# Nine half-chunk loads of a gated mix kernel, each as one transfer in place of two, under a new order of issue

## The chip, the cores and the metric

The kernel runs on one core of one Trainium2 chip. Times are device microseconds (us) of that core from start to end of an execution. Five engines work side by side, each on a list of instructions of its own that it takes strictly in order: PE (TensorE, matmuls), ACT (ScalarE), DVE (VectorE), POOL (GpSimd) and SP (SyncE, which here does nothing but issue transfers between the chip's memory and the on-chip memory of 128 partitions). Sixteen DMA engines carry out the transfers. Engines wait for each other and for transfers through semaphores. A lower time is better.

## The reference

Two branches over the same `x` (2048 rows of 640), mixed by a gate for each row:

```python
g = sigmoid((x * gate_w).sum(-1, keepdims=True))
# A: 32 heads of 20; each position attends to 8 positions back, two apart
qkv = x @ wqkv                      # 640 x 1920
a = softmax(q.k * scale over 8 positions) . v, then @ wo        # 640 x 640
# B: two dense layers with mish between them
h = x @ w1 + b1                     # 640 x 1728
b = (h * tanh(softplus(h))) @ w2    # 1728 x 640
out = g * a + (1 - g) * b
```

All of it is in float32. The hidden width of B is 1728 = 13 chunks of 128 and a last chunk of 64: that last half chunk is what the change is about.

## The kernel before, in words

**Arithmetic.** Every matmul operand is held as a pair of tiles, a high part (rounded) and a low part (what the rounding left), and every product is three matmuls: high by high, high by low, low by high (`mm3`, lines 522 to 524). The first layer of B, the projections and `wo` use a Strassen-like scheme of seven products in place of eight; the second layer (`mlp2`) does so over the halves of the hidden width and of the output: seven products `a b c e g d f`, each over seven chunks of the hidden width.

**What a load is.** A chunk (128 partitions by 256 to 512 columns, so 128 to 256 KB) is fetched by a transfer that SP issues, into a `raw`, `z` or `hb` buffer or straight into a `pair` buffer. ACT copies it to the high part (line 463). DVE or POOL subtracts to get the low part (line 466). Only then can PE read it. In the stretch of `mlp2` each step needs one chunk of weights and two of activations (`act`, `actt`, which the first layer has written to the chip's memory).

**The half chunk.** Products b, g and f end with a chunk of only FR = 64 rows. There the kernel puts the 64 rows twice into the 128 partitions and lets one matmul do the work of two: the high weights stand below the low ones, so two matmuls (lines 1401 and 1402) replace three. `load_low_w` fetches such weights (three times), `load_low_act` such activations (six times: products b, g, f by two halves P of the rows). Both fetch through `twice` (line 1199), which issues the same 64 rows as two transfers, one to partitions 0 to 63 and one to partitions 64 to 127 (line 1203). In `load_low_w`, line 1211 is ACT's high part, 1212 DVE's low part, 1214 the second copy by ACT and 1215 a clearing by POOL.

**What sets the order.** The code records 2856 tasks with their dependencies and buffers. A table written out by hand, `ISSUE`, gives for each of the five engines the order of its task numbers; a second table, `TAKEN`, gives for each ring of buffers which engine takes the next one. `Plan.run` walks the tables and emits the instructions in just that order; tasks marked for either engine run on DVE or POOL, whichever list they stand in. Nothing reorders afterwards. An engine that comes to a task whose inputs are not there waits, and all that stands behind it in its list waits too. SP's list is the order in which all transfers are issued.

**Other transfers that matter below.** `placed_unit` moves a border of the key and value tile by two transfers, one of 112 partitions and one of 15 (`kv[112:127]`), eight times for each of two widths. `make_gates` stores gates by transfers of 8 partitions, eight in all. All other transfers have 128, 64, 32 or 16 rows. In the program of before, the first dimension of a transfer is always its number of partitions or rows.

Of the kernel before, what the change touches and what calls it, by code (L numbers as in the profile page):

```python
# [22 lines left out]
FR = F - FC * 128  # L23
# [43 lines left out]
class Task:  # L67
# [8 lines left out]
    "PE": """1 96-110 115 120 125 135 130 145 140 244 240 236 232 290 263 302 294 267 298 376 377 380 381 383 385 425 426 386 429 387 430  # L76
487 432 434 488 435 491 456 436 492 494 496 468 464 497 498 460 540 548 544 536 619 620 623 624 626 628 650 629 630 651 654
655 657 659 681 660 724 661 725 728 689 729 693 685 731 733 734 767 735 759 755 763 878 921 894 922 925 1047 1046 1049 926
928 930-932 1048 1063 1089 1064 1090 1066 1092 1065 1107 1091 1108 1125 1109 1203 1204 1127 1110 1126 1207 1208 1128 1210
1212-1214 1234 1235 1338 1238 1339 1239 1241 1243-1245 1340 1289 1371 1341 1290 1372 1391 1373 1293 1294 1374 1392 1296 1298  # L80
1299 1394 1300 1459 1460 1393 1505 1463 1464 1506 1466 1468 1509 1469 1470 1510 1515 1517-1519 1542-1544 1559 1545 1560 1562
1583 1581 1561 1597 1595 1631 1582 1584 1632 1596 1633 1609 1611 1634 1598 1610 1612 1729 1658 1730 1657 1660 1880 1659 1732
1881 1731 1882-1891 1901 1902 1927 1928 1938 1939 1973-1984 2026-2037 2047 2048 2060 2061 2071 2072 2098-2109 2137-2144 2151
2152 2162 2163 2173 2174 2190-2197 2239-2246 2265 2266 2276 2277 2287 2288 2307-2314 2337-2348 2358 2359 2371 2372 2382 2383
2402-2413 2446-2457 2467 2468 2478 2479 2489 2490 2506-2517 2543-2550 2557 2558 2570-2573 2674 2574-2578 2675 2679 2579 2695
2580 2581 2680 2684 2696 2686 2700 2701 2689 2692 2705 2707 2806 2729 2710 2831 2733 2713 2807 2832 2811 2836 2828 2837 2812
2816 2841 2843 2818 2846 2821 2824 2849 2853""",
    "ACT": """7 4 10 13 19 16 31 22 25 28 47 38 41 35 44 116 126 111 62 127 121 78 74 122 59 117 118 136 112 50 72 123 128 131 119 228 124
# [12 lines left out]
1246 1237 1359 1367 1161 1388 1368 1248 1249 1257 1387 1004 1164 1375-1377 1369 1292 1291 1251 1378 1379 1007 1380 1381 1370  # L101
# [16 lines left out]
2779 2730 2734 2833 2781 2756 2785 2827 2753 2759 2789 2829 2787 2815 2840 2817 2842 2852 2854""",  # L118
    "DVE": """0 8 5 14 20 11 17 23 26 32 29 48 39 42 36 45 68-70 63 60 51 73 75 57 54 161 162 164 165 185 167 186 168 188 91 155 189 278
170 171 191 360 172-175 93 176 192 177 371 283 178 364 179 194-196 392 197 311 312 398 198 199 401 314 441 315 200 201 317  # L120
202 318 447 335 336 424 203 320 503 321-323 509 338 339 324-326 341 342 327 328 344 345 516 557 558 329 560 635 346 606 618
641 561 347 644 913 348 666 563 349 350 564 351 672 352 581 582 566 567 353 568 569 584 585 570 740 571 851 828 587 746 857
588 572-574 590 591 853 592 871 593 890 594 595 776 777 855 899 779 780 596 597 937 782 1056 575 598 943 800 1103 941 783
801 1121 954 785 786 599 787 963 803 788 804 789 790 806 791 807 792 993 793 1334 794 1027 1156 1219 1225 1157 1159 1346 809
810 1160 811 1018 1150 1354 1347 1355 1250 812 1162 1256 813 1356 1163 1348 814-816 1349 1165 817 1166 818 1167 1168 1357
1169 1170 1180 1305 1311 1181 1171 1183 1184 1172 1173 1412 1475 1481 1186 1187 1413 1174 1415 1416 1524 1529 1418 1189-1194
1419 1195-1197 1436 1640 1198 1636 1437 1421-1423 1638 1642 1637 1424-1426 1641 1639 1427 1643 1439 1440 1428 1951 1429 1430
1942 1666 1442 1842 1443 1852 1667 1669 1670 1445-1447 1931 1448-1454 1672 2004 2051 2040 1673 1690 1691 1995 1675 1998 1693
1676 1694 1677 1678 2043 1679-1681 2087 1696 1682 1683 1697 2124 2158 1750 1699 2147 2136 1700 1751 1701 1684 2155 2161 2150
1702 2294 2177 1703 1704 2207 2189 1705 2183 1753 1754 2272 2216 1706 2275 2283 1707 1756 2300 2094 2297 1708 1757 2333 2324  # L130
1774 1775 2327 1759 1760 2357 2351 1761 2598 2392 1762 2362 2330 2354 2224 2367 1763 2499 1764 2414 2561 2416 2389 2418 2381
# [198 lines left out]
def kernel(ctx: ExitStack, tc: tile.TileContext, x, wq, wo, w1, b1, w2, out):  # L330
    nc = tc.nc
# [59 lines left out]
    add = plan.add  # L391
# [808 lines left out]
    def twice(to, src, after=()):  # L1200
        def both():
            for a in (0, FR):
                nc.sync.dma_start(to.at(slice(a, a + FR)), src())
# [587 lines left out]
```

## Time and profile before

| what | value |
|---|---|
| time, median of 3 runs | 612.4 us (611.7 to 614.93) |
| time of the profiled execution | 615.71 us |
| its span, first to last instruction | 613.9 us |
| matmuls | 2645, granted clock 1.00 |
| PE busy | 605.7 us, 99% of the span |
| DVE, ACT, POOL busy | 566.4, 402.5, 396.2 us |
| bytes moved | 164.20 MB |
| transfers issued | 758 by SP, 12 by POOL |

The span is what the engines show; the 1.8 us between it and the time of that execution lie before the first and after the last instruction. The profiled execution was 3.3 us longer than the median. Rows of waits read "who waits <- whom: us in total, times, longest". Rows of a chain of waits read "start, length, what". Rows by stretch of time give, for each engine, its busy us and in brackets its number of instructions, then the granted clock, the mean busy share of the 16 DMA engines and GB/s. PE's busy time includes matmuls that are pipelined, so the count of matmuls in a stretch tells more of its pace than its busy time.

### The profile page before, as it was taken

The page shows a single profiled execution, that of the slowest core. Times are in us where ns is not written, and L with a number is a line of the kernel's source. Part 1 is how long each engine was busy: PE and PEld are TensorE (multiplying, and loading weights), DVE is VectorE, ACT ScalarE, POOL GpSimd, SP SyncE. Part 2 cuts the span into 40 slices and gives each one's busy share as a digit, 9 for nine tenths or more (in the row PEclk, how much of TensorE's full clock was granted, in tenths as well). Part 3 has the DMA queues.
Part 4 walks back from the last instruction along what each step waited for, and adds up shares of the span by engine and source line. Part 5 has one row for each costly group of instructions (what it writes and reads, how often), then busy time and mean ns, then how long its engine had stood idle before and what let it go on. Part 6 is the DMA issues. An engine that isn't in the chain of part 4 may idle for free.

```text
span 613.9 us, 9016 instructions
## 1 busy us (share of the span) xinstructions
PE 605.7 (99%) x2645; PEld 495.3 (81%) x2645; DVE 566.4 (92%) x513; ACT 402.5 (66%) x902; POOL 396.2 (65%) x355
## 2 busy tenths in 40 slices
PE   9999999999999999999999999999999999999997
PEld 6888888888887888888788888878787778888886
DVE  4579999999999999899999999999999999998863
ACT  5745765677668687777779688376776565574631
POOL 1455574867987963687878798868756464524361
PEclk9999999999999999999999999999999999999999
DMA  9654666599988889999999999999999999998724
GB/s 308 213 161 124 163 198 226 183 297 311 320 273 258 269 233 304 303 286 312 315 327 301 302 287 266 272 269 286 289 325 317 334 333 336 338 332 253 248 69 154
DMA packets 109009, 164.20 MB, mean 267 GB/s; under 512 B 12432, under 2 KB 55952, under 8 KB 108928
## 3 DMA queue, kind: packets, MB, share of 16 engines
q1 hardware_dynamic: 107616, 161.28, 82.1%
q0 software_dynamic: 1344, 2.36, 2.6%
q8 instruction: 20, 0.33, 0.2%
q14 instruction: 29, 0.24, 0.1%
HBM read 95.81 MB, written 59.98 MB: 254 GB/s over the span
## 4 chain that ended last, share of the span: by engine, by line
PE 72%; DVE 11%; DMA 9%; issue 4%; POOL 2%; ACT 1%; SPq 1%; DVEq 0%; POOLq 0%; ACTq 0%
PE bank L522 23%; PE bank L524 23%; PE bank L523 23%; DMA pair<-act 4%; DVE pr L613 2%; DMA pair<-s 2%; DVE kvq L622 2%; DVE lg L578 1%; DMA raw<-in_w 1%; DVE pr L575 1%; POOL pair L466 1%; PE bank L664 1%; DMA actt<-hb 1%; PE bank L446 1%; DMA raw<-in_x 1%
## 5 line engine op out<-in xcount | busy, mean ns | idle before, releaser
L522 PE MATMUL bank<-pair,pair 128*128 128x512 f32 (+2 forms) x710 | 276.2, 389 | 2.6 <-ACT kvq L1300 1.2
L523 PE MATMUL bank<-pair,pair 128*128 128x512 f32 (+2 forms) x710 | 276.5, 389 | 0.3 <-POOL pair L466 0.2
L524 PE MATMUL bank<-pair,pair 128*128 128x512 f32 (+2 forms) x710 | 275.8, 388 | 0.3 <-POOL pair L466 0.2
L522 PEld LDWEIGHTS bank<-pair,pair 128*128 128x128 f32 x710 | 133.3, 188 | 31.5 <-ACT kvq L1300 1.7
L523 PEld LDWEIGHTS bank<-pair,pair 128*128 128x128 f32 x710 | 133.4, 188 | 29.5 <-POOL pair L466 2.3
L524 PEld LDWEIGHTS bank<-pair,pair 128*128 128x128 f32 x710 | 133.4, 188 | 28.8 <-POOL pair L466 2.4
L466 POOL TENSOR_TENSOR pair<-pair 128x512 fp32r<-128x512 f32 (+3 forms) x86 | 108.2, 1273 | 54.6 <-DVE pair L466 19.7
L466 POOL TENSOR_TENSOR pair<-raw,pair 128x512 fp32r<-128x512 f32 (+4 forms) x88 | 109.7, 1257 | 36.2 <-ACT pair L463 14.0
L463 ACT ACTIVATE pair<-pair 128x512 fp32r<-128x512 f32 (+3 forms) x155 | 89.7, 612 | 51.0 <-DMA pair<-act 18.5
L575 DVE TENSOR_TENSOR pr<-kvq,side 128x2560 f32<-128x2560 f32 x32 | 90.0, 2813 | 5.2 <-ACT side L581 4.2
L463 ACT ACTIVATE pair<-raw 128x512 fp32r<-128x512 f32 (+4 forms) x121 | 72.9, 617 | 31.3 <-POOL raw L950 7.2
L613 DVE TENSOR_TENSOR pr<-kvq,side 128x2560 f32<-128x2560 f32 x32 | 90.2, 2819 | 0.7
L622 DVE TENSOR_REDUCE kvq<-pr 128x320 f32<-128x2560 f32 x32 | 90.1, 2815 | 0.6
L578 DVE TENSOR_REDUCE lg<-pr 128x128 f32<-128x2560 f32 x32 | 89.9, 2810 | 0.6
L950 POOL TENSOR_TENSOR raw<-raw,raw 128x256 f32<-128x256 f32 (+3 forms) x53 | 57.6, 1089 | 36.3 <-DVE pair L466 16.8
L466 DVE TENSOR_TENSOR pair<-pair 128x512 fp32r<-128x512 f32 (+4 forms) x69 | 48.1, 729 | 2.0 <-ACT pair L463 2.0
L670 ACT ACTIVATE kvq<-bank 128x320 f32<-128x320 f32 x64 | 27.6, 436 | 24.5 <-PE bank L524 24.3
L522 PE MATMUL bank<-kvq,pair 128*128 128x512 f32 x102 | 40.1, 393 | 0.0
L524 PE MATMUL bank<-kvq,pair 128*128 128x512 f32 x102 | 39.9, 391 | 0.0
L523 PE MATMUL bank<-kvq,pair 128*128 128x512 f32 x102 | 39.8, 390 | 0.0
L466 DVE TENSOR_TENSOR pair<-raw,pair 128x512 fp32r<-128x512 f32 (+2 forms) x33 | 24.0, 745 | 7.7 <-ACT pair L463 7.5
L1097 ACT ACTIVATE bank<-bank 128x512 f32<-128x512 f32 x36 | 21.1, 588 | 8.0 <-PE bank L524 7.8
(138 smaller groups left out, 710.8 us busy)
## 6 DMA issues: line engine op xcount, KB each, us to landing
pair<-actt SPq DMA_DIRECT2D x54, 256.0 KB, 4.5
pair<-act SPq DMA_DIRECT2D x38, 256.0 KB, 4.6
raw<-in_w SPq DMA_DIRECT2D x34, 256.0 KB, 4.5
raw<-in_wq SPq DMA_DIRECT2D x34, 248.0 KB, 4.1
raw<-in_x SPq DMA_DIRECT2D x29, 256.0 KB, 4.8
actt<-hb SPq DMA_DIRECT2D x28, 256.0 KB, 3.7
act<-z SPq DMA_DIRECT2D x24, 256.0 KB, 4.0
actt<-z SPq DMA_DIRECT2D x24, 256.0 KB, 3.9
```

The lines of the kernel that those rows point to most:

```text
L463: a = add("ACT", act_ns(n), lambda: A.activation(hi(), raw(), AF.Copy), after, rank=rank, take=take, hold=hold, kind="hi")
L466: return (V if e == "DVE" else G).tensor_tensor(lo(), raw(), hi().bitcast(F32), op=OP.subtract)
L522: nc.tensor.matmul(ps, ah, bh, start=first, stop=False, skip_group_check=more)
L523: nc.tensor.matmul(ps, ah, bl, start=False, stop=False, skip_group_check=more)
L524: nc.tensor.matmul(ps, al, bh, start=False, stop=last, skip_group_check=more)
L575: return V.tensor_tensor(pr, window(kv, s0, 0), qs[:, :, None, :].to_broadcast([128, 2, W, QF]), op=OP.mult)
L578: return V.tensor_reduce(lg_w[:, s0:s0 + 2], pr.rearrange("p s w (h d) -> p s w h d", d=DH), op=OP.add, axis=AX.X)
L613: return V.tensor_tensor(twos, vw, pw[:, :, :, :, None, None].to_broadcast([128, 2, W, HQ, DH // 2, 2]), op=OP.mult)
L622: return step("DVE", 2740, lambda: V.tensor_reduce(q[:, s0:s0 + 2].rearrange("p s (f j) -> p f s j", j=2), by_place, op=OP.add, axis=AX.X) ...
L670: a = add("ACT", 330, lambda: A.activation(kv[:, 7 + s], ps.t[:, QF:3 * QF].rearrange("p (a b) -> p a b", a=2), AF.Copy), [done] + before, ...
L950: return (V if e == "DVE" else G).tensor_tensor(t.t[:, i:i + n], a.t[:, j:j + n], b.t[:, k:k + n], op=op)
L1097: return add("ACT", 590, lambda: A.activation(to.t, of.t, AF.Copy), after, rank=-0.6, take=[to], hold=[of], kind=kind)
```

## The change

Two things change. First, `twice` issues one transfer to all 128 partitions, whose source names the 64 rows two times: a first dimension of size 2 and step 0 is put ahead of the 64 rows. Second, both tables are replaced: the order of tasks on all five engines, and with it which of DVE and POOL does a task (88 tasks change sides, 44 each way). The tasks themselves, their 2645 matmuls, and what they compute stay; SP issues 749 transfers in place of 758.

```diff
 TAKEN / ISSUE: every list is another permutation of the same 2856 task numbers, e.g. of SP's first row
-    "SP": """6 3 9 12 18 21 15 30 24 215 214 46 27 43 40 37 34 65 33 66 64 61 49 58 67 55 52 150 151 217 80-82 208 152 273 153 222 211
+    "SP": """3 6 12 9 215 18 214 15 37 21 24 30 27 46 34 40 43 49 65 61 58 64 66 67 52 151 55 150 221 33 217 81 80 211 208 223 222 152
...
     def twice(to, src, after=()):
-        def both():
-            for a in (0, FR):
-                nc.sync.dma_start(to.at(slice(a, a + FR)), src())
-
-        return [add("SP", 900, both, after, take=to.take, size=to.n * 820)]
+        return [dma(to.at, lambda: src()[None, :, :].to_broadcast([2, FR, to.n]),
+                    after, take=to.take, size=to.n * 512)]
```

Lines behind `twice` move up by three: line 1211 of before is line 1208 of the change, 1300 is 1297, 1231 is 1228; the transfers of `twice` now carry the line of the common helper, 472.

Three pieces of the lists, first SP's before, at products g and f, some 470 us into the execution. A row names line, operation, target, source and the target's shape; `act22_0_6` is the half chunk (the seventh, so 6) of the activations for product g, P = 0, `s6` its weights, `in_w2` the half chunk of weights for product f:

```order
L1203 DMA pair5_4806<-act22_0_6_119 64x512 x2
L472 DMA pair9_4816<-act22_1_3_123 128x512
L1203 DMA pair0_4822<-s6_189 64x384 x2
L472 DMA pair17_4834<-s5_188 128x384
L472 DMA pair1_4841<-act22_1_2_122 128x512
L472 DMA pair11_4845<-actt3_1_1_163 128x512
L472 DMA os1_1_296<-raw2_4740 128x512
L1203 DMA hb0_4863<-in_w2 64x256 x2
```

The same place in the change; `128x1x512` marks the new transfers:

```order
L472 DMA pair15_4815<-act22_0_6_119 128x1x512
L472 DMA pair0_4822<-act22_0_3_116 128x512
L472 DMA hb0_4828<-in_w2 128x1x256
L472 DMA pair5_4835<-act22_1_5_125 128x512
L472 DMA pair12_4867<-s6_189 128x1x384
L1228 DMA raw3_4869<-in_w2 128x256 x2
L472 DMA os1_1_296<-raw1_4572 128x512
L472 DMA pair3_4877<-act22_0_5_118 128x512
```

Three of the nine half chunks stood within eight entries (eleven transfers) and now stand within five; loads of whole chunks for product g (`act22_1_5`, `act22_0_5`) stand right behind them.

ACT's list before, some 405 us into the execution, at the end of product a. `kvq1<-bank` at line 1300 are the copies of finished products out of the matmul banks, which PE waits for before it opens these banks again:

```order
L905 ACT_TABLE_LOAD
L905 ACTIVATE pair8_3968<-pair8_3968,bias_77 64x512
L1211 ACTIVATE pair19_4169<-hb1_4122 128x384
L1300 ACTIVATE kvq1_221<-bank0_63 128x512
L463 ACTIVATE pair21_4105<-pair21_4105 128x512
L1300 ACTIVATE kvq1_221<-bank6_69 128x512
```

and in the change:

```order
L463 ACTIVATE pair12_4059<-pair12_4059 128x512
L1208 ACTIVATE pair20_4163<-hb1_4132 128x384
L1297 ACTIVATE kvq1_221<-bank5_68 128x512
L1297 ACTIVATE kvq1_221<-bank0_63 128x512
L463 ACTIVATE pair4_4108<-pair4_4108 128x512
L1297 ACTIVATE kvq1_221<-bank3_66 128x512
```

The high part of product b's half chunk of weights still stands just ahead of the first copy out of a bank; a table load and one activation that stood ahead of it have gone to a later place.

More of the change, by code (lines that the diff above doesn't have):

```diff
@@ L75 @@
 ISSUE = {
[L76 to L83, printed above, removed]
@@ L84 @@
-2152 2162 2163 2173 2174 2190-2197 2239-2246 2265 2266 2276 2277 2287 2288 2307-2314 2337-2348 2358 2359 2371 2372 2382 2383
[L85 to L88, printed above, removed]
[12 rows of a table removed]
@@ L101 @@
-1246 1237 1359 1367 1161 1388 1368 1248 1249 1257 1387 1004 1164 1375-1377 1369 1292 1291 1251 1378 1379 1007 1380 1381 1370
[16 rows of a table removed]
[L118 to L130, printed above, removed]
@@ L131 @@
-1774 1775 2327 1759 1760 2357 2351 1761 2598 2392 1762 2362 2330 2354 2224 2367 1763 2499 1764 2414 2561 2416 2389 2418 2381
-1777 1778 1765 2395 2398 1766 2482 2428 2420 1780 1767 2437 2257 2443 1768 2536 1781 2460 2463 2471 2258 2474 1783-1785 2259
[3 rows of a table removed]
-2754 2786 2834 2795 2770 2774 2835 2788 2838 2802 2803 2844 2809 2813 2819 2810 2825 2850 2822 2847""",
-    "POOL": """216 2 79 218 219 71 77 84 85 210 86 229 220 95 213 225 274 231 227 276 277 89 87 287 362 363 289 271 285 259 375 253 409 369
[6 rows of a table removed]
-1799 1608 1805 1838 1534 1646 1039 1814 1652 1649 1635 1535 1808 1811 1868 1817 1802 1533 1869-1871 1915 1823 1916 1917 1820
[4 rows of a table removed]
@@ L149 @@
-2662 2663 2643 2666 2718 2724 2796 2752 2798 2772 2757 2784 2760 2804 2790 2800 2792 2794 2805""",
-    "SP": """6 3 9 12 18 21 15 30 24 215 214 46 27 43 40 37 34 65 33 66 64 61 49 58 67 55 52 150 151 217 80-82 208 152 273 153 222 211
[5 rows of a table removed]
-750 357 1122 1101 678 1332 845 1086 881 880 885 743 865 748 1060 773 1054 1057 952 774 897 934 752 1335 579 1119 901-903
-1036 961 754 577 945 578 955 576 942 940 900 1097 157 1098 958 947 904 988 949 997 985 951 1861 982 991 1146 1116 601-603
[19 rows of a table removed]
-2848 2855""",
+    "PE": """1 96-110 115 120 125 130 145 135 140 244 236 290 232 263 267 294 240 302 298 376 377 380 381 425 383 385 386 426 387 429 487
@@ new lines @@
+430 432 434 488 491 492 435 436 456 494 464 496 497 468 460 498 540 548 536 544 619 620 623 624 650 626 628 629 651 630 654
+655 657 659 681 660 661 724 725 728 689 685 729 731 733 693 734 735 755 767 759 763 878 921 894 922 925 1047 1046 1049 926
+928 930-932 1048 1063 1089 1090 1066 1064 1107 1091 1108 1092 1065 1125 1109 1203 1204 1110 1127 1126 1207 1208 1128 1210
+1212-1214 1234 1338 1235 1238 1339 1239 1241 1243-1245 1340 1341 1289 1371 1372 1290 1373 1391 1293 1294 1374 1392 1296 1298
+1393 1299 1300 1459 1394 1505 1460 1506 1509 1463 1464 1466 1468-1470 1510 1515 1517-1519 1545 1542-1544 1559 1581 1560 1582
@@ new lines @@
+1562 1584 1561 1583 1595 1597 1631 1609 1611 1633 1596 1598 1634 1632 1612 1729 1610 1657 1660 1880 1731 1658 1730 1659 1881
+1882 1732 1883-1891 1901 1902 1927 1928 1938 1939 1973-1984 2026-2037 2047 2048 2060 2061 2071 2072 2098-2109 2137-2144 2151
+2152 2162 2163 2173 2174 2190-2197 2239-2246 2265 2266 2276 2277 2287 2288 2307-2314 2337-2348 2358 2359 2371 2372 2382 2383
+2402-2413 2446-2457 2467 2468 2478 2479 2489 2490 2506-2517 2543-2550 2557 2558 2570-2572 2674 2573-2578 2695 2675 2579-2581
@@ new lines @@
+2679 2680 2696 2684 2700 2701 2686 2689 2705 2692 2707 2806 2729 2710 2713 2733 2831 2807 2832 2811 2836 2837 2828 2812 2841
+2843 2816 2818 2846 2849 2821 2824 2853""",
+    "ACT": """4 7 13 10 19 16 38 22 25 28 47 31 35 41 44 59 116 78 117 118 121 126 62 111 72 122 123 146 112 131 50 132 133 147 127 119
[14 rows of a table added]
+1401 1402 1400 1287 1403 1304 1404-1406 1507 1182 1312 1461 1537 1281 1306 1307 1462 1465 1033 1185 1467 1471 1576 1514 1540
+1557 1473 1474 1411 1482 1476 1019 1516 1551 1414 1188 1477 1508 1579 1554 1511 1546 1801 1834 1520 1417 1525 1547 1549 1497
@@ new lines @@
+1526 1563 1564 1521 1530 1565 1435 1593 1548 1629 1420 1804 1572 1585 1607 1626 1587 1573 1574 1604 1566 1599 1798 1567 1601
+1586 1438 1568-1571 1645 1648 1613 1653 1614 1588 1837 1600 1810 1619 1615 1919 1620 1602 1725 1651 1656 1622 1840 1623 1616
+1621 1907 1950 1624 1713 1727 1617 1714 1715 1654 1722 1665 1723 1733 1655 1724 1726 1941 1618 1739 1734 1807 1716 1831 1736
+1735 1728 1737 1719 1816 1740 1717 1718 1720 1441 1819 1721 1741 1822 1742-1744 1738 1825 1944 2003 1828 1904 1893 1668 1444
[9 rows of a table added]
@@ new lines @@
+2777 2734 2781 2785 2765 2833 2827 2789 2840 2787 2829 2815 2842 2852 2817 2854""",
+    "DVE": """0 8 5 14 11 216 20 17 26 23 39 29 48 32 42 45 36 68 69 60 79 63 219 51 57 54 161 162 164 165 213 274 185 89 186 87 188 167
+168 155 189 170-174 191 175 192 363 176-178 194-197 311 179 392 312 398 198 199 401 441 314 315 250 200 447 418 201 317 318
+202 335 336 320 503 321 338 322 203 339 509 323-325 341 342 326 512 327 422 328 344 557 558 560 708 345 635 329 561 641 346
+347 644 913 348 666 349 350 563 351 672 564 352 353 581 582 566-569 584 585 570 571 740 857 572 587 746 588 851 828 573 574
@@ new lines @@
+590-592 871 593 853 890 594 595 776 777 855 899 779 780 596 597 937 782 1056 575 943 598 1103 783 800 954 801 1121 599 803
+948 785-788 804 950 789 790 978 1027 791 963 792-794 987 806 1156 1219 807 990 1225 1157 1346 1159 1354 1347 809 810 1160
+811 812 1150 1355 1250 1162 1256 1163 813 1356 1348 814 815 1165 816 1349 817 818 1166 1167 1357 1180 1168 1181 1169 1170
+1305 1311 1171 1183 1184 1172 1173 1475 1186 1187 1481 1412 1174 1413 1415 1524 1416 1189 1190 1529 1191-1193 1418 1419
+1194-1196 1421 1422 1197 1436 1198 1636 1640 1437 1642 1638 1423-1425 1639 1637 1643 1426 1641 1439 1440 1951 1427-1430 1666
@@ new lines @@
+1442 1852 1842 1443 1942 1667 1669 1445 2040 1446 1670 1447-1450 1931 1451-1454 2004 2051 1672 1673 1690 1691 1995 2015 1998
+1675 1676 1693 1677 1678 1694 1966 2043 1679-1683 1696 2133 2136 1697 2124 2087 1750 2158 2090 1751 2092 1699-1701 2155 1702
+2189 2150 2294 2161 1703 1684 1704 2183 2207 1753 1754 2216 1705 2272 1706 1756 2275 2283 1707 1708 2297 2598 1757 2333 2094
+2223 1774 1775 2324 2362 2321 2327 2367 1759 2499 1760-1762 2351 2234 2330 1763 2392 2354 2395 1764 2414 2416 2418 2389 1777
@@ new lines @@
+2482 1778 2398 1765 2536 2431 1766 2631 2437 1780 1767 2443 2420 1768 2474 2460 2561 2463 2471 1781 2258 2485 2502 2477 2259
+1783-1788 2533 2496 2610 1789 1790 2556 2601 1791 2604 2616 2542 2526 2566 2640 2521 2607 2569 1792 2594 2625 2628 2613 2655
+2597 2664 2622 2658 2591 2634 2662 2672 2660 2671 2681 2637 2673 2677 2678 2646 2663 2727 2736 2702 2668 2666 2690 2698 2687
+2724 2708 2693 2767 2699 2768 2764 2769 2711 2762 2780 2778 2772 2773 2754 2796 2782 2766 2757 2834 2804 2714 2835 2795 2788
@@ new lines @@
+2794 2809 2802 2800 2838 2792 2810 2819 2844 2847 2813 2850 2822 2825""",
+    "POOL": """218 2 70 71 73 77 220 75 227 84 210 229 85 276 86 95 91 278 287 225 360 231 362 93 271 277 283 259 373 364 369 371 289 285
+409 411 375 262 253 396 256 413 403 520 405 424 522 475 523 412 445 450 476 533 477 478 452 524 529 454 531 507 514 516 535
+609 705 615 707 420 612 480 699 618 718 639 606 914 915 709 646 714 720 916 716 968-970 648 971 670 675 825 677 843 679 846
+840 847 848 702 834 723 863 831 837 744 866 749 884 860 867 868 1042 873 1045 849 893 869 877 887 875 898 751 1059 1062 1088
@@ new lines @@
+1085 753 1106 1124 941 946 960 1337 957 1334 999 993 996 981 984 1015 1223 1228 1016 1017 1230 1232 1363 1269 1018 1366 1360
+1270 1254 1259 1271 1261 1002 1272 1005 1008 1324-1326 1279 1011 1591 1285 1288 1263 1309 1327 1282 1314 1316 1493 1538 1318
+1577 1558 1494 1479 1020 1541 1484 1495 1552 1486 1555 1038 1580 1037 1496 1488 1594 1523 1498 1630 1835 1608 1627 1605 1799
+1649 1646 1838 1533 1534 1652 1039 1802 1868 1635 1869-1871 1811 1814 1535 1841 1808 1805 1908 1817 1915 1820 1823 1826 1829
[4 rows of a table added]
@@ L178 @@
+2652 2748 2746 2718 2752 2750 2776 2771 2798 2784 2770 2786 2774 2790 2760 2803 2805""",
+    "SP": """3 6 12 9 215 18 214 15 37 21 24 30 27 46 34 40 43 49 65 61 58 64 66 67 52 151 55 150 221 33 217 81 80 211 208 223 222 152
[26 rows of a table added]
+2826 2823 2814 2855""",
 }
 TAKEN = {
-    "bank": ("0000000000000000000000010110101010101001000000101100110100100101000000100010010111100111000101101011100111111100101"
-        "011110100101100100111101110000011110000100111010010111011101100111111"),
-    "raw": ("4444444434444444444444444444434442444444344444434444444444344444444444444444444444444444444444441444144444444444444"
-        "444444444444444444444444441444144444444444444444444443444444434424424444411444444444"),
@@ L184 @@
-    "pair": ("1111111111111111111111111111111111111111111111111111111111141141111111141414111411211111441111111141121111141114111"
-        "4111144111441414441441411441441411214424411444114144414444444444444444444444144444441444444444444444444444444444441"
-        "44444144444444441441444444444444144444414444444444444444444444441111441111"),
+    "bank": ("0000000000000000000000010101011011001010000000101010110100101001000000100000110111100111001010100111010111111010011"
+        "011110000111100110011101101000011110000100111001001111011110100111111"),
@@ new lines @@
+    "raw": ("4444424444444444444444444444244444434444344444434444444443444444444444444444444444444444444444414444144444444444444"
+        "444444444444444444444444444411444444444444444444444442444444434444224444414144444444"),
+    "pair": ("1111111111111111111111111111111111111111111111111111111111114114111111141414141111211111414111121111141111141141111"
+        "4111411414141444141414141444141141421442114444141144144444444444444441444444444144444444444444444444444444444444441"
+        "41444444441444444414444444144444444414444444444444444444444444411414141111"),
@@ L187 @@
     "hb": ("44441111111111111111111111411411111111444424144"),
-    "z": ("441212121212121211141124124412121211114442414444444"),
+    "z": ("441212121212121211114124142412121211114442414444444"),
 }
```

118 rows, old and new, of the table ISSUE are left out of this document.

## Prediction

> **What bounds the kernel now.** I read the page first: engines, DMA, packets.
>
> ```profile
> PE 605.7 (99%) x2645; PEld 495.3 (81%) x2645; DVE 566.4 (92%) x513; ACT 402.5 (66%) x902; POOL 396.2 (65%) x355
> DMA  9654666599988889999999999999999999998724
> DMA packets 109009, 164.20 MB, mean 267 GB/s; under 512 B 12432, under 2 KB 55952, under 8 KB 108928
> ```
>
> PE is the bound, and the change leaves its 2645 matmuls as they are: time can only come from or go into gaps between them. The DMA engines are at 9 tenths or more from the middle on. So I went on to stretches of 25 us over the second layer, where all nine half chunks are fetched.
>
> ```profile
> core 0: us, PE busy (x) PEld busy (x) DVE busy (x) ACT busy (x) POOL busy (x), PEclk, DMA share, GB/s
> 400.00:425.00 25.00, 23.75 (x105) 19.37 (x104) 22.93 (x20) 17.13 (x30) 18.36 (x21) 1.00 0.98 270
> 425.00:450.00 25.00, 24.31 (x104) 19.04 (x104) 24.25 (x25) 20.51 (x43) 17.06 (x17) 1.00 0.95 302
> 450.00:475.00 25.00, 24.90 (x106) 19.13 (x105) 24.52 (x20) 16.00 (x34) 17.32 (x15) 1.00 0.98 322
> 475.00:500.00 25.00, 24.98 (x110) 20.16 (x109) 24.30 (x28) 11.94 (x25) 14.09 (x15) 1.00 1.00 332
> 500.00:525.00 25.00, 24.79 (x108) 19.94 (x108) 24.86 (x28) 16.15 (x35) 13.76 (x11) 1.00 0.99 339
> 525.00:550.00 25.00, 25.00 (x111) 20.64 (x110) 24.97 (x29) 15.97 (x31) 10.79 (x9) 1.00 1.00 327
> ```
>
> The last row, 111 matmuls in 25 us (0.225 us each), is PE without gaps. Against it the five others lack 6, 7, 5, 1 and 3, 22 matmuls or 5.0 us. That is about all that a better order could win here, and part of it is this execution's own: it took 615.71 us (span 613.9), 3.3 us above the median of 612.4. I make the sum as a difference and add it to the median. The DMA share in these rows is 0.95 to 1.00: the idle part is (0.02+0.05+0.02+0+0.01+0) x 25 = 2.5 us in 150. Then the chain of waits from 460 us on, and ACT's timeline in the same place:
>
> ```profile
> 463.49 6.44 DMA pair<-act
> 469.95 0.52 SPq L1203
> 470.51 4.52 DMA pair<-act
> 475.05 0.49 SPq L1203
> 475.65 5.41 DMA pair<-s
> 481.12 4.63 DMA pair<-act
> 485.78 0.63 ACT pair L463
> ```
>
> ```profile
> 478.52 1.20 ACT L463 ACTIVATE pair<-pair 128x512 fp32r<-128x512 f32 x2 [2.30 <-DMA pair<-act]
> 480.04 1.55 ACT L463 ACTIVATE pair<-pair 128x384 fp32r<-128x384 f32 x3
> 485.78 0.63 ACT L463 ACTIVATE pair<-pair 128x512 fp32r<-128x512 f32 x1 [0.70 <-DMA pair<-act]
> ```
>
> Transfer follows transfer on the chain for 22 us, and ACT stands idle until loads land (2.30 and 0.70 us) and splits them at once. In this stretch loads come just in time. What lands later here is soon PE's wait.
>
> **The change part by part: the transfers.** Before, the nine loads are 18 transfers:
>
> ```profile
> L1203 SPq DMA_DIRECT2D pair<-act x8: 457/474/594, 400.3 to 486.1; - x8
> L1203 SPq DMA_DIRECT2D hb<-in_w x4: 480/506/1182, 397.4 to 475.0; - x4
> L1203 SPq DMA_DIRECT2D pair<-actt x4: 444/452/587, 532.8 to 537.4; - x4
> L1203 SPq DMA_DIRECT2D pair<-s x2: 445/520/594, 471.2 to 471.7; - x2
> DMA to landing us min/median/max: 4.0/5.0/5.8
> ```
>
> *Removed:* nine issues of about 0.5 us on SP. Two of these stretches lie on the chain above (0.52 and 0.49 us), so 0.5 us each could leave it: 1 us at most, and I take 0.5.
>
> *Added:* nothing in bytes. But how a transfer is dealt to the 16 engines can be counted in this trace. The DMA view's 78 groups (first and last below) sum to 758 transfers on SP and 12 on POOL.
>
> ```profile
> pair<-actt SPq DMA_DIRECT2D x54, 256.0 KB, 4.5
> kvq<-kvq SPq DMA_DIRECT2D x8, 75.0 KB, 3.7
> kvq<-kvq SPq DMA_DIRECT2D x8, 56.2 KB, 3.9
> g<-gt SPq DMA_DIRECT2D x8, 1.0 KB
> bias<-in_b SPq DMA_DIRECT2D x1, 7.0 KB, 4.7
> ```
>
> The page has 12432 packets under 512 B. Data of that size are the 128 rows of the bias and 8 x 8 rows of the gates: 192. The other 12240 are the words that engines write to the semaphore when their part has landed. If every engine that takes part writes one, then 758 + 12 - 16 - 8 = 746 transfers on 16 engines give 11936, the sixteen transfers of 15 partitions (75.0 and 56.2 KB) on 15 engines give 240, the eight of 8 partitions on 8 give 64: 12240, to the packet. So a transfer whose first dimension is under 16 runs on that many engines only. The new transfer's source has a first dimension of 2. By the same counting it runs on **two** engines, with 64 rows on each.
>
> [...]
>
> *Price.* At 332 GB/s with a share of 1.00 (475 to 500 us) one engine moves 20.75 GB/s, a row of 2048 B in 98.7 ns. Sixteen engines with 8 rows each: 0.79 us. Two with 64 each: 6.32 us. The difference, 5.5 us, is what these two engines owe for one half chunk of activations, and any later transfer needs its share of these two engines before it has landed. Weights by width: 384 columns 5.5 x 0.75 = 4.1 us, 256 columns 2.8 us. Six activations, two wide weights, one narrow: 33.2 + 8.3 + 2.8 = **44 us**. The lower bound of the price is 0 or the 1 us gained (rival A); I take 44 because the counted rows are of the same kind as the new one.
>
> *Cover.* First the idle share, 2.5 us. Then the lead that loads have. The half chunks stand in six occasions: three single ones for product b (397 to 421 us), three together for g and f (469 to 475), one at 486, two for f (533 to 537). At each, the lead is between 0 (the rows with 2.30 and 0.70 us, where ACT waits for the landing) and 6 to 7 us (the activations issued at 469.35 us, with 5.0 us to landing, are split in the group that begins at 480.04, ACT's queue holding them up). I take the middle, 3.3 us, six times: 20. Left on PE's path: 44 - 2.5 - 20 - 0.5 = **21 us**. Bounds: with no lead 41 us, with 6.6 us each time 1 us or so.
>
> **The order.** At 405 us ACT's copy out of the bank waits behind the split of b's half chunk of weights:
>
> ```profile
> 405.06 0.52 ACT pair L1211
> ```
>
> and PE's longest wait there, from the list of waits (total us, times, longest):
>
> ```profile
> PE bank L522 <- ACT kvq L1300: 1.2, 1, 1.2
> ```
>
> The change drops a table load ahead of that split but leaves the split ahead of the copy. If its load, issued at 397.4, lands 4.1 us later than its 5 us, that is 406.5, and the 1.2 us of PE's wait become more, not less. At 470 us the three half chunks move together: on two engines that is 5.5 + 4.1 + 2.8 = 12.4 us of arrears at once, with product g's own whole chunks behind them. For the rest (all lists, 44 tasks each way between DVE and POOL, whose work of 566 and 396 us stays about as it is) the trace tells no sign. Bounds: the 5.0 us of lacking matmuls won back, or as much again lost. I take 0.
>
> **The forecast:** 612.4 + 21 = 633 us, slower by 3.4%. Its own range, from occasions that are mostly covered to no cover and a lucky order: 618 to 655.
>
> **Rivals.** *A: all 16 engines* (the source's two dimensions merged, or the target's 128 deciding). For: the target has 128 partitions first, and the change then does what it says. Against: a source of 8 or 15 rows decided before, though there both sides were small. Then nothing is owed, 1 us of issue leaves the chain and the order wins some of the 5 us: 612.4 - 0.5 - 1.5 = 610, between 607.5 and 614. It ends faster or the same. Chance 0.22: 0.10 faster, 0.12 the same.
>
> *B: two engines, but hidden.* The order would have to give six occasions 7 us of lead each. For: some loads do lie 10 us in their buffers, and PE has work of other products mixed in. Against: the chain above and shares near 1.00, since arrears on full engines do not drain. About 614, 612 to 617. Chance 0.16: 0.11 the same, 0.05 slower.
>
> *C: worse than the sum.* SP itself blocks behind the arrears, so that stores and loads of other work come late and DVE (97% in these rows) cannot catch up: 44 us and some, 655 to 670. It decides once a single arrears of 12 us empties all `pair` buffers. Chance 0.07, slower.
>
> **How the numbers follow.** Likeliest 0.55, slower. What this kernel's measurement can tell from no change is about 0.5%, 3 us. Faster by more: 0.10; within: 0.12 + 0.11 = 0.23; slower: 0.55 + 0.05 + 0.07 = 0.67. The range reaches down to A's middle and up to the likeliest's end: 610 to 655; it leaves out half of A and C, 0.11 + 0.07 = 0.18. The likeliest's own stands above, 618 to 655.
>
> **What would show it.** Packets under 512 B: 12432 - 18 x 16 = 12144, plus 9 x 2 = 12162 for two engines, plus 9 x 16 = 12288 for sixteen: this decides A. The new transfers' landing: 10 us or more in place of 5.0. The 25 us rows from 400 us on: matmuls well under 104 in at least three of them and GB/s under 300, as fourteen engines idle while two work off arrears; ACT's waits for `pair<-act` and `pair<-actt` longer than 5 us. PE's stretches before 395 us should be the same as now. I am wrong if the landing stays at 5 us, or if it grows and PE's counts do not fall.

## The result and the profile after

The changed kernel takes **646.6 us** (median of 4, 641.56 to 647.6) against 612.7 us of the kernel before in the same session: a ratio of 1.0516, 95% interval 1.0472 to 1.0559. It is slower by 5.2%, 34 us. Forecast were 633 us, 610 to 655.

The profiled execution has a span of 645.2 us, 31.3 us more than before. From its page the matmuls' busy time, the granted clock by slices, and the packets:

```profile
PE 613.8 (95%) x2645; PEld 502.7 (78%) x2645; DVE 566.6 (88%) x513; ACT 403.0 (62%) x902; POOL 400.5 (62%) x355
...
PEclk9999999999998999999999999797999799999999
...
DMA packets 108739, 164.20 MB, mean 254 GB/s; under 512 B 12162, under 2 KB 55682, under 8 KB 108658
```

The same 2645 matmuls and the same bytes. The packets under 512 B are 12162, the number that the prediction gave for two engines, to the packet. And the clock row, all 9 before, now has three 7s (and an 8 in the slice from 194 us on, of which the last section tells).

The stretches of 25 us from 400 us on, after:

```profile
400.00:425.00 25.00, 21.23 (x83) 17.04 (x82) 20.71 (x20) 13.56 (x27) 13.45 (x14) 0.86 0.80 220
425.00:450.00 25.00, 19.06 (x71) 14.95 (x70) 17.26 (x13) 13.98 (x30) 15.75 (x16) 0.86 0.78 225
450.00:475.00 25.00, 25.00 (x112) 20.68 (x111) 24.36 (x23) 16.21 (x32) 16.91 (x15) 1.00 0.93 308
475.00:500.00 25.00, 21.33 (x93) 17.01 (x91) 17.66 (x17) 9.85 (x23) 12.72 (x12) 1.00 0.75 233
500.00:525.00 25.00, 19.57 (x72) 15.02 (x73) 18.83 (x22) 11.44 (x23) 12.01 (x10) 0.86 0.72 227
525.00:550.00 25.00, 25.00 (x111) 20.68 (x112) 24.82 (x31) 13.48 (x29) 11.73 (x10) 1.00 0.99 341
550.00:575.00 25.00, 22.32 (x95) 17.27 (x93) 20.03 (x19) 13.76 (x27) 10.11 (x9) 1.00 0.75 236
575.00:600.00 25.00, 22.49 (x90) 17.95 (x91) 22.07 (x31) 13.89 (x25) 9.48 (x9) 0.93 0.96 328
```

Where matmuls lack (83, 71, 93, 72, 95, 90), the bytes per second lack too (220 to 236 GB/s but for the last row), and the two rows between these occasions are full. All of the loss lies here. One stretch of 400 us and one of 200 us, of before and then of after, say so:

```profile
0.00:400.00 400.00, 397.85 (x1747) 327.85 (x1748) 374.75 (x305) 278.44 (x662) 280.82 (x253) 1.00 0.85 262
400.00:600.00 200.00, 197.74 (x856) 159.35 (x855) 186.64 (x202) 122.32 (x237) 114.72 (x103) 1.00 0.89 285
```

```profile
0.00:400.00 400.00, 396.47 (x1746) 328.26 (x1747) 373.70 (x306) 281.32 (x662) 281.35 (x252) 1.00 0.85 262
400.00:600.00 200.00, 176.01 (x720) 140.60 (x719) 165.73 (x170) 106.17 (x213) 102.16 (x92) 0.94 0.83 265
```

Up to 400 us the two kernels differ by one matmul. Between 400 and 600 us, 136 matmuls are missing: at 0.225 us each 30.6 us, of the 31.3 us by which the span grew.

The chain of waits names the transfers (start, length, what). Parts of it, after:

```profile
398.86 8.92 DMA hb<-in_w
407.83 0.41 issue
408.24 0.59 ACT kvq L1297
...
425.48 10.26 DMA pair<-act
...
490.65 11.82 DMA pair<-s
...
567.40 9.21 DMA o<-ot
```

The first three rows of transfers are three of the nine half chunks: weights of product b, activations of b, weights of g. They take 9 to 12 us where half chunks took 4.0 to 5.8 before. The last is an ordinary transfer, issued behind the half chunks of product f, and it is held up as long. The first is the place of the prediction's ACT list: until b's weights land at 407.8 us, their split on ACT cannot begin, and the copy out of a bank (the row of 408.24), for which PE waits, stands behind the split.

Now PE at the four longest stops. The list alternates: a stop, and the stretch right behind it (columns as above, the bracket behind PE is the count of matmuls):

```profile
404.72:408.87 4.15, 0.38 (x2) 0.00 (x1) 0.64 (x2) 1.06 (x3) 0.00 (x0) 0.81 0.90 235
408.87:414.29 5.42, 5.42 (x13) 4.29 (x14) 5.32 (x5) 5.39 (x9) 4.68 (x5) 0.52 0.84 233
432.26:439.09 6.83, 0.89 (x3) 0.19 (x1) 0.71 (x1) 3.25 (x7) 2.54 (x3) 0.92 0.40 107
439.09:444.97 5.88, 5.88 (x14) 4.62 (x15) 5.81 (x4) 3.85 (x11) 5.88 (x6) 0.51 0.99 284
497.25:504.30 7.05, 0.39 (x2) 0.00 (x1) 1.17 (x3) 1.86 (x5) 0.00 (x0) 0.90 0.59 176
504.30:509.79 5.49, 5.49 (x13) 4.33 (x14) 5.35 (x10) 3.87 (x9) 3.69 (x3) 0.51 0.86 294
572.72:578.32 5.60, 1.20 (x5) 0.30 (x3) 2.28 (x4) 2.78 (x5) 1.27 (x1) 0.96 0.62 192
578.32:581.58 3.26, 3.26 (x8) 2.64 (x9) 3.26 (x6) 0.91 (x2) 0.00 (x0) 0.54 0.99 355
```

Behind each stop PE is busy without a gap, but at a granted clock of 0.51 to 0.54, and a matmul takes about 0.42 us in place of 0.225. The four stops lack 3.7 + 6.2 + 6.6 + 4.5 = 20.9 us (their length less their matmuls at 0.225 us). The four stretches behind them lose 2.5 + 2.7 + 2.6 + 1.5 = 9.3 us more, without any wait. So the loss has two parts: late loads, and the half clock that the stops bring with them.

### The profile page after: what moved, and what is told of

Same layout as the page of the kernel before. It is cut to its first block, busy times and chain, and to the rows that moved or that the text cites. A ratio compares the mean times of both kernels' runs of the same rounds, so it can differ in the third digit from the quotient of the medians.

```text
span 645.2 us, 8996 instructions
## 1 busy us (share of the span) xinstructions
PE 613.8 (95%) x2645; PEld 502.7 (78%) x2645; DVE 566.6 (88%) x513; ACT 403.0 (62%) x902; POOL 400.5 (62%) x355
## 2 busy tenths in 40 slices
DMA packets 108739, 164.20 MB, mean 254 GB/s; under 512 B 12162, under 2 KB 55682, under 8 KB 108658
## 4 chain that ended last, share of the span: by engine, by line
PE 69%; DMA 12%; DVE 9%; POOL 3%; ACT 3%; issue 2%; SPq 1%; DVEq 0%; POOLq 0%; ACTq 0%
PE bank L524 22%; PE bank L523 22%; PE bank L522 22%; DVE pr L575 3%; DMA pair<-s 3%; POOL pair L466 2%; DVE lg L578 2%; DMA pair<-act 2%; SPq L472 1%; DMA o<-ot 1%; DMA hb<-in_w 1%; DVE kvq L622 1%; DVE pr L613 1%; PE bank L664 1%; ACT pair L463 1%
## 5 line engine op out<-in xcount | busy, mean ns | idle before, releaser
L522 PE MATMUL bank<-pair,pair 128*128 128x512 f32 (+2 forms) x710 | 279.1, 393 | 12.3 <-ACT kvq L1297 5.1
L524 PE MATMUL bank<-pair,pair 128*128 128x512 f32 (+2 forms) x710 | 278.8, 393 | 6.7 <-DVE pair L466 6.7
L523 PE MATMUL bank<-pair,pair 128*128 128x512 f32 (+2 forms) x710 | 279.5, 394 | 2.0 <-POOL pair L466 1.2
L466 POOL TENSOR_TENSOR pair<-pair 128x512 fp32r<-128x512 f32 (+4 forms) x90 | 114.9, 1292 | 87.3 <-ACT pair L463 29.8
L522 PEld LDWEIGHTS bank<-pair,pair 128*128 128x128 f32 x710 | 135.5, 191 | 42.5 <-ACT kvq L1297 5.9
L524 PEld LDWEIGHTS bank<-pair,pair 128*128 128x128 f32 x710 | 135.4, 191 | 34.4 <-DVE pair L466 7.4
L523 PEld LDWEIGHTS bank<-pair,pair 128*128 128x128 f32 x710 | 135.3, 191 | 31.0 <-DVE pair L466 2.0
L466 POOL TENSOR_TENSOR pair<-raw,pair 128x512 fp32r<-128x512 f32 (+4 forms) x89 | 112.1, 1269 | 57.5 <-ACT pair L463 20.3
L463 ACT ACTIVATE pair<-pair 128x512 fp32r<-128x512 f32 (+4 forms) x155 | 89.6, 612 | 68.7 <-DMA pair<-act 28.9
L463 ACT ACTIVATE pair<-raw 128x512 fp32r<-128x512 f32 (+3 forms) x121 | 72.8, 618 | 23.0 <-POOL raw L950 6.8
L950 POOL TENSOR_TENSOR raw<-raw,raw 128x512 f32<-128x512 f32 (+3 forms) x55 | 60.2, 1096 | 40.4 <-DVE pair L466 12.0
L466 DVE TENSOR_TENSOR pair<-pair 128x512 fp32r<-128x512 f32 (+2 forms) x65 | 47.9, 763 | 8.7 <-ACT pair L463 8.6
L466 DVE TENSOR_TENSOR pair<-raw,pair 128x512 fp32r<-128x512 f32 (+3 forms) x32 | 22.3, 706 | 15.2 <-ACT pair L463 15.2
```

The costliest lines, as they stand in the source:

```text
L463: a = add("ACT", act_ns(n), lambda: A.activation(hi(), raw(), AF.Copy), after, rank=rank, take=take, hold=hold, kind="hi")
L466: return (V if e == "DVE" else G).tensor_tensor(lo(), raw(), hi().bitcast(F32), op=OP.subtract)
L522: nc.tensor.matmul(ps, ah, bh, start=first, stop=False, skip_group_check=more)
L523: nc.tensor.matmul(ps, ah, bl, start=False, stop=False, skip_group_check=more)
L524: nc.tensor.matmul(ps, al, bh, start=False, stop=last, skip_group_check=more)
L950: return (V if e == "DVE" else G).tensor_tensor(t.t[:, i:i + n], a.t[:, j:j + n], b.t[:, k:k + n], op=op)
```

## The experiments

Two theories stood against each other at first. **Arrears:** the first dimension of 2 puts a transfer on two engines, which then hold up all later transfers. **Order:** the new tables make the loss, whatever the transfers.

### One part of the change at a time

The tables of before with the new `twice`:

```diff
...
-        return [add("SP", 900, both, after, take=to.take, size=to.n * 820)]
+        return [dma(to.at, lambda: src()[None, :, :].to_broadcast([2, FR, to.n]),
+                    after, take=to.take, size=to.n * 512)]
```

> The tables of before with the new transfer (source of 2 x 64 rows) in all nine places. Theory, two engines and their arrears: about as slow as the change, 640 to 655 us, with 12162 packets under 512 B, since the transfer alone makes the loss. Rival, the new order makes the loss: 611 to 615 us, as before.

Measured: 639.2 us (636.9 to 639.81), a little under the 640 to 655 us that I expected; ratio 1.043, interval 1.0397 to 1.0463. Its packets:

```profile
DMA packets 108739, 164.20 MB, mean 257 GB/s; under 512 B 12162, under 2 KB 55682, under 8 KB 108658
```

And the reverse, the tables of the change with the old pair of transfers:

> The tables of the change with the old pair of 64-row transfers in all nine places. Theory of two engines: 608 to 616 us, 12432 packets under 512 B, no stretch of 25 us between 400 and 575 us with under 100 matmuls. Rival, the new order makes the loss: 640 us or more.

Measured: 612.7 us (611.47 to 617.36), ratio 1.000, interval 0.9969 to 1.0031. Its stretch from 400 to 600 us:

```profile
400.00:600.00 200.00, 199.70 (x875) 163.12 (x874) 186.25 (x204) 119.64 (x236) 118.53 (x104) 1.00 0.88 283
```

The transfer alone makes the loss; the order alone makes none and wins none (between 400 and 600 us its trace has 19 matmuls more than that of before, 4.3 us, but the profiled execution of before was itself 3.3 us above its median, and the medians come out even). But they are not independent. With the new transfer the old order loses 4.3% and the new one 5.2%, with intervals that do not overlap: the new tables, which put three half chunks within five entries of SP's list, stand the arrears less well.

### The number of engines

With the tables of the change, a transfer of the same bytes whose first dimension is 16, 8 or 4 (one line for the three kernels, with k in place of their numbers):

```diff
-        src()[None, :, :].to_broadcast([2, FR, to.n])
+        src()[:128 // k][None, :, :].to_broadcast([k, 128 // k, to.n])   # k = 16, 8, 4
```

> The tables of the change; each of the nine transfers names the first 8 of its rows sixteen times (first dimension 16, step 0) in place of 64 rows twice. The operands of the half chunks are then other numbers: part of the computation is changed, bytes and shapes of the transfer are not. Theory, the size of the first dimension sets how many engines work: 12288 packets under 512 B and 606 to 614 us. Rival, any source with step 0 is slow, or a single transfer to 128 partitions is: 640 us or more. Rival, the order: 640 us or more.

> The tables of the change; each of the nine transfers names the first 16 of its rows eight times (first dimension 8). Part of the computation is changed as in the run with sixteen. Eight engines, 12216 packets under 512 B, 16 x 98.7 ns = 1.6 us for activations in place of 0.8: the nine owe 44 x 0.79 / 5.5 = 6.3 us, which the lead of the loads hides. Theory: 611 to 616 us. Rival, what an engine owes is paid in full whatever its size: 619 us.

> The tables of the change; each of the nine transfers names the first 32 of its rows four times (first dimension 4). Part of the computation is changed as in the run with sixteen. Theory: four engines, 12180 packets under 512 B; one half chunk of activations takes 32 x 98.7 ns = 3.2 us in place of 0.8, the nine owe 44 x 2.4 / 5.5 = 19 us in place of 44, most of it inside the lead that loads have: 613 to 628 us. Rival, the loss is a fixed price of the form and not of the number of engines: 640 us or more, as the change.

| first dimension | packets under 512 B | owed by the nine, us (estimate from 98.7 ns a row) | median, us | ratio to before, interval |
|---|---|---|---|---|
| 16 | 12288 | 0 | 613.2 | 0.9998 (0.9977 to 1.0018) |
| 8 | 12216 | 6.3 | 615.5 | 1.0028 (0.9983 to 1.0072) |
| 4 | 12180 | 19 | 624.2 | 1.0186 (1.0153 to 1.022) |
| 2 (the change) | 12162 | 44 | 646.6 | 1.0516 (1.0472 to 1.0559) |

The page of the kernel with 16:

```profile
DMA packets 108865, 164.20 MB, mean 269 GB/s; under 512 B 12288, under 2 KB 55808, under 8 KB 108784
```

The packets are 12144 plus nine times the first dimension, to the packet, which is the count of as many engines as the first dimension says; and the time follows it. Neither the step of 0 nor the single transfer to 128 partitions costs anything: with 16 engines the kernel is where it was (613.2 us, ratio 0.9998). It is not ahead either. So the nine issues that the change saves are worth nothing, and rival A's gain of 2 us did not come with all engines at work either. From 4 to 2 engines the owed time grows 2.3-fold and the loss 3-fold (11 to 34 us): it looks as if the lead of the loads covered a part of fixed size, and all above it were paid, with the clock on top; this is an argument from four points, no run shows it by itself. At 8 engines the measurement does not tell the 2 us from nothing.

### Which engines

If each transfer took the next two engines in turn, two in a row would spread over four. So each half chunk again as two transfers to the two halves of the partitions, each with a first dimension of 2:

```diff
...
+            for a in (0, FR):
+                nc.sync.dma_start(to.at(slice(a, a + FR)), src()[:32][None, :, :].to_broadcast([2, 32, to.n]))
...
```

> The tables of the change; each half chunk again as two 64-row transfers, each of which names the first 32 of its rows twice (first dimension 2). Part of the computation is changed. 12180 packets under 512 B. If a transfer of first dimension 2 always goes to the same two engines, these owe as much as in the change: 638 to 650 us. If the next transfer goes on to the next two engines, four share the work as in the run with four: 616 to 630 us.

Measured: 646.8 us (645.15 to 651.74), ratio 1.0547 (1.0487 to 1.0606). It names four times 32 rows in all, as the kernel with first dimension 4 does, and has the same 12180 packets, yet it is 23 us slower than that one and as slow as the change. So in these kernels the two engines are the same two each time: had the next two worked in turn, the estimate was 616 to 630 us. That is why the arrears of neighbouring half chunks add up. The trace of the change shows it from the other side, in the single steps of the semaphores that tell of landings: the first half chunk, issued at 398.86 us, lands in two steps, at 407.23 and 407.79 us, where an ordinary chunk lands in sixteen; and of an ordinary chunk issued at 403.94 us, behind it, all parts but two have landed by 408.67 us, and the last two come at 410.75 and 411.24 us.

### Weights and activations apart

With the tables of the change, only the three half chunks of weights as one transfer, and then only the six of activations:

```diff
...
+        if to.inner and to.n == 512:      # in the second kernel: if to.n < 512
+            return [add("SP", 900, both, after, take=to.take, size=to.n * 820)]
...
```

> The tables of the change; only the three half chunks of weights by the new transfer (2 x 64 rows), the six of activations by the old pair of transfers. They owe 11 of the 44 us of the two engines. Theory, each occasion pays by itself as the chain of the changed kernel shows it (stops of 4.2 us behind b's weights and 7.1 us behind g's, each with a stretch of half clock after it): 619 to 630 us. Rival, only arrears that add up over several half chunks show: 612 to 616 us.

> The tables of the change; only the six half chunks of activations by the new transfer, the three of weights by the old pair. They owe 33 of the 44 us. Theory, each occasion pays by itself (stops of 6.8 us behind b's activations and 4.7 us around f's, with half clock after them): 625 to 637 us, and the losses of this run and of the run with the weights alone come to about the 34 us of the change. Rival, arrears that add up: 638 us or more here, nothing with the weights alone.

Measured, against 612.4 us of before: weights 623.6 us (ratio 1.0181, 1.0117 to 1.0246), activations 636.2 us (1.0382, 1.0332 to 1.0433). The losses are 11.2 and 23.8 us; their sum of 35.0 us is that of the change, 33.9. Each group pays its own. The three weights owe 11 us and pay 11, the six activations owe 33 and pay 24. A single cover of 3.3 us for each occasion, as the prediction had it, is therefore an average that fits neither group: the weights had next to no cover. The longest stop with the weights alone is the one at 406 us, where the copy out of the bank waits behind their split.

### The clock by itself

If a long stop costs clock, the same total of stops must cost more in few long pieces than in many short ones. In the kernel before, ScalarE's copy of a bank, for which PE waits, is done again n times (the result is the same):

```diff
...
+            for _ in range(self.pause.get(id(t), 0)):   # four tasks: 8; in the other kernel fourteen tasks: 3
+                t.fn()
             t.ins = ins = t.fn(e) if t.both else t.fn()
```

> The kernel of before with four made stops of PE: at four copies of a bank by ScalarE that PE waits for (at about 68, 132, 251 and 321 us) the same copy is done eight times more, which by their 0.6 us and the slack there is 4 x 4.3 = 17 us of stop in all. Theory, a stop of over about 4 us is followed by a stretch at half clock (0.43 us for a matmul in place of 0.23, some 12 matmuls each): 17 + 4 x 2.5 = 27 us over before, 635 to 645 us, and rows with a granted clock under 1 behind each stop. Rival, a stop costs its own length only: 626 to 632 us, the clock at 1.00.

> The kernel of before with fourteen made stops of PE, each by three more copies of a bank (1.8 us less the slack there, 1.3 us on average), 18 us in all, about as much as in the run with four long stops. Theory, short stops do not touch the clock: 18 us over before or a little less where later waits are absorbed, 624 to 632 us, no row with a granted clock under 1 outside the first 10 us. Rival, any stop costs clock: as slow as four long stops or slower.

Measured, against 612.4 us: four long stops 639.9 us (ratio 1.0444, 1.0386 to 1.0502), fourteen short ones 630.8 us (1.03, 1.0245 to 1.0356). The losses are 27.5 and 18.4 us. Two of the four long stops, each with what follows it:

```profile
69.17:73.78 4.61, 0.39 (x3) 0.01 (x1) 2.96 (x2) 4.39 (x9) 3.60 (x4) 0.81 0.58 145
73.78:79.00 5.22, 5.22 (x13) 4.12 (x14) 3.17 (x3) 4.26 (x11) 1.05 (x1) 0.51 0.44 84
139.33:143.93 4.60, 0.39 (x3) 0.01 (x1) 0.88 (x2) 4.38 (x9) 1.23 (x1) 0.98 0.95 323
143.93:148.00 4.07, 4.07 (x11) 3.25 (x12) 3.52 (x2) 2.12 (x6) 2.49 (x2) 0.61 0.14 52
```

And stretches with short stops in the other kernel:

```profile
68.00:73.00 5.00, 3.85 (x17) 2.89 (x16) 4.36 (x6) 4.87 (x11) 3.63 (x4) 1.00 0.54 155
260.00:265.00 5.00, 3.52 (x16) 2.60 (x15) 3.14 (x2) 3.33 (x11) 1.62 (x2) 1.00 0.90 277
414.00:420.00 6.00, 3.88 (x13) 2.43 (x11) 5.79 (x8) 5.81 (x11) 3.82 (x6) 0.82 0.96 294
```

Two kernels with about 18 us of stops each differ by 9 us. Behind all four long stops the clock falls (0.51 and 0.61 above, 0.63 and 0.58 behind the other two), and PE's 48 matmuls in these four stretches of 18.0 us take 7.2 us longer than at 0.225 us each: most of the 9. My expectation for the short stops was wrong in one detail: one of the fourteen, at 415 us, also came with a lower clock (0.82 over the 6 us of the last row, PE busy for 3.88 of them). In the page's clock row, in slices of 15.7 us, this is the only one that is not 9.

Behind all eight long stops, the four of the change and the four made ones, the traces show a granted clock of 0.51 to 0.63 over the next 3.3 to 5.9 us; a stop of about 2 us they show with and without a lower clock behind it (the last section).

## Why the prediction was right, and where its sum was short

**The count of engines** (12162 packets, forecast for two engines, 12288 for sixteen): right to the packet, as all the counts of the other kernels. It was read off transfers of 15 and 8 rows, and the counts with first dimension 2, 4, 8 and 16 (12162, 12180, 12216, 12288) follow it.

**The price** (5.5 us for a half chunk of activations on each of two engines, 44 us in all): nothing contradicts it; the landing of 10 us or more that it asked for is 8.9, 10.3 and 11.8 us on the chain, and the loss grows with it from 8 to 2 engines.

**The cover** (23 of 44 us, so 21 us left on PE's path): right in size, and in part by luck: 3.3 us was the middle between 0 and 6 to 7, and the weights alone paid all of the 11 us that they owe. The four long stops lack 20.9 us. What else is lost there, by the starts of the matmuls in the trace, is about 6 us in stops of up to 2 us, and the kernel before had 5 us of such stops.

**The missing term: the clock.** The sum took a matmul at 0.225 us throughout, since the table showed a granted clock of 1.00. It priced stops at their own length. The runs show 9.3 us in the four stretches behind the stops, and 9 us between the kernels with long and with short stops. Forecast 21 us, measured 34: 9 of the 13 us are this. Of the other 4, 1 us is the difference in the stops of up to 2 us, and 3 us come from the executions that were compared: the spans of the two traces differ by 31.3 us and not by 34, since the profiled execution of before was 3.3 us above its median. The likeliest case's own range of 618 to 655 held the time only because its bounds for the cover were wide, not because the clock was thought of.

**The order** (taken as 0, with bounds of 5 us won or lost): right where loads come in time, 612.7 against 613.5 us. Under arrears the new tables lose about 5 us more than the old ones (5.2% against 4.3%). These 5 us are no term beside the others: between 400 and 600 us the trace of the old tables with the new transfer has 749 matmuls at a granted clock of 0.96, that of the change 720 at 0.94, so they lie in the same stops and the same half clock. A sign for it stood in the prediction, though no run tries it alone: the three half chunks of g and f together, with product g's whole chunks behind them.

**The removed issues** (0.5 us): 0 within the measurement, by the kernel with sixteen engines.

**The rivals.** A fell with the count. B (hidden) fell with PE's counts. C put the time at 655 to 670 us because SP itself would block. The loss is not that large, but SP does block. Its issues in order of time behind the half chunks of g and f:

```profile
482.80 1.22 SPq L472 DMA_DIRECT2D pair<-act  x2
484.49 0.57 SPq L472 DMA_DIRECT2D hb<-in_w  x1
485.17 5.38 SPq L472 DMA_DIRECT2D pair<-act  x1
490.65 0.53 SPq L472 DMA_DIRECT2D pair<-s  x1
```

The first row has one new transfer, the second is the next; the issue after them, of an ordinary chunk, takes 5.38 us in place of 0.4, and the third new transfer, whose landing PE waits for at 504 us, can only be issued behind it. In the kernel with old transfers and the new order no issue between 395 and 585 us takes over 2 us. I had given SP's blocking a place only in the case of 655 us and more; it also occurs in the likeliest case. But the loss does not need it: with two transfers of two engines, as slow as the change (646.8 us), the longest issue there takes 2.75 us. What the 5.38 us cost is not shown.

Of what was to show it, one thing did not come: ACT's waits for `pair<-actt` stay under 5 us (longest 3.6), those for `pair<-act` reach 8.2.

## What to carry to other kernels

Look at the first dimension of a transfer's source as well as of its target: with 8, 4 and 2 the packets here (12216, 12180, 12162) are those of only so many DMA engines, with 2 the same two each time (646.8 us with two such transfers for each half chunk, 646.6 us with one), and what was issued afterwards waited for them (the last two parts of an ordinary chunk landed 2.1 and 2.6 us behind the other fourteen). Two plain transfers of 64 rows cost less than one that repeats 64 rows twice (612.7 against 646.6 us), and nine saved issues were worth nothing here (613.2 us with first dimension 16, 613.5 us before). When a change will make the matmul engine stop for more than about 4 us at a time, add to the stop some 2 us for the matmuls at half clock behind it, an estimate from the eight long stops above (1.5 to 2.7 us behind each).

## What was not expected of the hardware

**Half clock after a stop.** All eight long stops of PE above (4.15 to 7.05 us in the change, 4.60 to 4.68 us in the kernel with four made stops) are followed by it. A shorter one goes both ways: the same wait of about 2 us, between 192 and 196 us, is followed by a granted clock of 0.57 in the kernel with the new order and two transfers and of 1.00 in the one with first dimension 16:

```profile
194.50:198.50 4.00, 4.00 (x11) 3.15 (x12) 3.16 (x2) 3.97 (x11) 2.34 (x2) 0.57 0.69 262
```

```profile
195.70:199.50 3.80, 3.80 (x17) 3.11 (x18) 2.94 (x2) 3.80 (x11) 2.11 (x2) 1.00 0.68 256
```

No kernel was made to find out what decides it, but the clock records of the change's trace tell something. Its half clock (0.50) comes in pieces of 3.41 us, one or two in a row. Such runs of pieces begin at 195.63, 407.26, 437.98, 502.83 and 577.92 us, which is 62, 9, 19 and 22 pieces from one to the next. So between these times every change of the clock in this trace falls on one grid of steps of 3.41 us. Two stretches of that length around the wait of above, with two transfers and then with first dimension 16:

```profile
191.59:195.00 3.41, 1.61 (x7) 1.05 (x6) 2.29 (x6) 3.38 (x9) 0.91 (x1) 1.00 1.03 292
195.00:198.41 3.41, 3.41 (x9) 2.65 (x8) 3.07 (x2) 3.41 (x9) 2.25 (x2) 0.50 0.66 250
```

```profile
191.55:194.96 3.41, 2.28 (x11) 1.61 (x9) 3.34 (x7) 2.43 (x3) 2.17 (x2) 1.00 1.00 256
194.96:198.38 3.42, 2.70 (x12) 2.21 (x13) 2.03 (x3) 3.42 (x13) 0.99 (x1) 1.00 0.95 362
```

In the first kernel the wait lies inside the first row, PE is busy for 1.61 of its 3.41 us, and the second row is granted 0.50. In the second kernel the wait is spread over both rows, PE is busy for 2.28 and 2.70 us, and the clock stays at 1.00. Counted along the clock records' grid from 12 us on, in the traces of the change and of before: five stretches at full clock are followed by half clock, and PE was busy for at most 1.6 us in each of them. 344 are not, and there PE was busy for 2.0 us or more, but for two (1.50 and 1.63 us, in the change). So in these two traces half clock came where PE had stood idle for about half of one stretch of 3.41 us or more, though not each time. That a wait of about 2 us gets it or not by where it lies on the grid fits the rows above; no run shows it by itself.

**An issue that takes 5.4 us.** SP's issue of an ordinary transfer stretched from 0.4 to 5.38 us behind half chunks on two engines. What it waits for inside is not shown.
